# Key products of steps 1 and 2 in one 64-column matmul a unit, with ScalarE copying the diagonal blocks

## The chip, the cores and the metric

One core of a Trainium2 chip runs the whole program. The metric is device time in microseconds (us), the median of repeated runs. The kernel before takes 965.38 us (three runs, 963.65 to 966.08). The profile is of one execution of 968.78 us, whose span from first to last instruction is 967.1 us.

## The reference

Three stages follow each other: a delta-rule attention over 768 tokens (4 batches, 8 heads, head size 48), a two-layer network with a squared relu (384 to 2048 to 384), and a maxout network (three 384 to 768 products, their maximum, then 768 to 384). All in fp32.

```python
k_n = k / (np.linalg.norm(k, axis=-1, keepdims=True) + 1e-06)
for t in range(S):
    kt, vt, bt = (k_n[:, :, t], v[:, :, t], beta[:, :, t, None])
    y[:, :, t] = np.einsum('bhd,bhde->bhe', q[:, :, t], state)
    v_old = np.einsum('bhde,bhd->bhe', state, kt)
    state = state + bt[:, :, :, None] * np.einsum('bhd,bhe->bhde', kt, vt - v_old)
...
g = np.maximum(x @ w_in, 0.0) ** 2 ; x = g @ w_out
h = np.maximum(np.maximum(x @ w1, x @ w2), x @ w3) ; out = h @ w_out2
```

## The kernel before

The 768 tokens are cut into six steps t = 0 to 5 of 128 tokens, and each step into two chunks of 64. Heads go in pairs; a pair and a chunk make a unit, 32 units a step. The attention of a step is four functions. `gram(t)` forms, for each unit, the 64x64 products of the chunk's keys with each other (into the tile G) and of keys with queries (masked, into W). `solve(t)` inverts a triangular system made of G, nearly all on VectorE, with a few 32x32 matmuls at its end. `values(t)` loads v and k and scales v. `chain(t)` carries the state from chunk to chunk and writes the attention's output (`outputs`), which `split` divides into a high and a low part, xh and xl. Then `moe1(t)` runs the relu network on the step's 512 columns (four batches of 128 tokens): `hidden` with the weights wih and wil, `project` with gh, gl and the weights wo, three reduced-precision (F32R) matmuls in place of each fp32 one. In step 0 the weights are loaded raw and split into high and low parts by ScalarE and VectorE (`load_w`, tiles raw and word), and wo is written out to DRAM (wod) to be read back in later steps. The maxout network comes last.

In steps 0 to 2 (`t < BLOCKS`) `gram` loads tokens whole, transposes them on TensorE (`features`: matmuls with ident, two of 64 rows per pair), copies the result from PSUM into W on ScalarE, and makes the products eight units at a time (a batch: four batches a step). The key product of a unit is made there as two matmuls with 32 stationary columns each, the second with its two moving halves swapped, so that the diagonal 32x32 blocks of the product land in columns 0 to 31 of both row halves; that is the layout `solve` wants. Beside it stands the query product with 64 stationary columns. In steps 3 to 5 `gram` reads k and q in blocks, transposes on VectorE, and makes the key product as one 64-column matmul; ScalarE then copies the blocks of partitions 32 to 63 and 96 to 127 into place, in two pieces of up to 256 columns. Key and query products of a batch go to two PSUM banks (pk and pq), from a ring of two banks in steps 1 and 2 (ps4 and ps5, numbered ps_90 and ps_91 in the rows). The key bank is free again when ScalarE has copied it, the query bank when VectorE has multiplied it with the mask. An fp32 matmul appears as two MATMUL instructions in the trace, as one in the program's rows.

The order on each engine is a list written at build time by the `Planner`: every instruction has a due time (`pl.at`, set from tables such as GL, CL, GRAM, SOLVE, CHAIN), and a list scheduler with costs orders each engine's queue, which the engine then works off strictly in that order. So a waiting instruction holds back everything behind it on its engine. All instructions are issued from one helper line, L369; they are told apart by their tiles.

Of the kernel before, what the change touches and what calls it, by code (L numbers as in the profile page):

```python
# [53 lines left out]
class Planner:  # L54
# [3 lines left out]

    MIX, FULL, STAY, BURST, URGENT = 0.1, 21.39, 23.78, 28.69, -2.83
    INTO, BACK, RUSH = 0.12, 0.24, 3.919
    HOLD = {"vector": 0.072, "sync": 4.88}
    CHUNK, SUPPLY, AHEAD = 256, 4.0, 64
    EVENT, LANES = 0.065, 8
    LAG = {"tensor": 0.2, "vector": 0.13, "scalar": 0.15, "gpsimd": 0.08, "sync": 0.0}

# [51 lines left out]
    def forward(self, at):  # L119
# [23 lines left out]
        while todo:  # L143
# [13 lines left out]
            r = ready.get(e, [])  # L157
            hold, later = self.HOLD.get(e, 0.0), []
            while r and r[0][0] <= t + (max(self.RUSH, hold) if hold else 0.0):
# [215 lines left out]
def kernel(  # L375
# [41 lines left out]
    GB = B // 2  # L417
    EPS = 1e-6

    GL, CL, G1, DEC, BOOST, SPL, CUT, HALF, G2, LATE, BLOCKS, FIRST, HURRY = -417, 491, -55, 1170, 2515, 58, 6, 8, -218, 228, 3, 0, 0  # L420
    GRAM = (-918, 367, -1037, 1518, 303, -975)
    SOLVE = (785, -3, -777, 1402, -1665, -543)
    CHAIN = (-867, -934, 2043, 294, 401, 966)
    TICKS = 6 * NF
    W_MIN, W_MAX = 2.0 ** -15, 122876.0

# [80 lines left out]
    def tok(t, b):  # L507
        return b if t == 0 else (t * B + b) % 2
# [11 lines left out]
    def load_blocks(t, c):  # L520

        for src, dst in zip((k, q), blocks):
            sv = src.rearrange("b (a j) (t h r) d -> j t h r (b a) d", j=2, h=2, r=32)
            for h in range(2):
                for j in range(2):
                    for f0, n in ((0, 32), (32, 16)):
                        for pairs, turn in parts(t, c):
                            p0 = 64 * (j ^ turn) + f0
                            pl.sync.dma_start(
                                out=dst[p0:p0 + 32, pairs, h, 0:n],  # L530
                                in_=sv[j, 2 * t + c, h, :, pairs, f0:f0 + n],
                            )

    def load_tok(t, b, pairs=((k, kt), (q, qt))):
        i = tok(t, b)
        for src, dst in pairs:
            n = 64 if turned(t, 1, b // 2) else P
            pl.sync.dma_start(
                out=dst[i].rearrange("p a j d -> p (a j) d")[0:n, :, 0:D],
                in_=src[b, :, t * P:t * P + n, :].rearrange("h s d -> s h d"),  # L540
            )
            for j in range(2) if n < P else ():
                pl.sync.dma_start(
                    out=dst[i][n:P, :, 1 - j, 0:D],
                    in_=src[b, j:H:2, t * P + n:(t + 1) * P, :].rearrange("h s d -> s h d"),
                )
# [41 lines left out]
    def adv(n):  # L588
        pl.at += n

    def gram(t, at):

        pl.at = at + GRAM[t]
        W, G = W2[t % 2], GG[t % 2]
        a_ring = gram_ring if t > 1 else Ring(banks[4:6] if t else banks)
        def features(b, keys):
            u0, u1 = 2 * HP * b, 2 * HP * (b + 1)
            ps = a_ring().rearrange("p (a x) -> p a x", a=HP)
            src = (kt if keys else qt)[tok(t, b)]
            for a in range(HP):  # L600
                pl.tensor.transpose(
                    ps[:, a, :], src[:, a].rearrange("p j d -> p (j d)"), ident
                )
            ps = ps.rearrange("p a (c x) -> p (a c) x", c=2)
            if keys:
                pl.scalar.activation(W[:, u0:u1, 0:64], ps, AF.Copy)
            else:
                pl.scalar.activation(W[0:64, u0:u1, 64:128], ps[0:64], AF.Copy)
                pl.scalar.activation(W[64:128, u0:u1, 128:192], ps[64:128], AF.Copy)

        def products(units, keys, queries):

            n = 2 * HP
            Wu, Gu = (x[:, units] for x in (W, G))
            pk, pq = (a_ring().rearrange("p (u x) -> p u x", u=n) if x else None for x in (keys, queries))
            for x in range(n):
                with pl.together(beside=True):
                    for p0, q0, c0 in ((0, 64, 64), (64, 0, 128)):
                        key = Wu[p0:p0 + 64, x, 0:64]
                        if keys and t < BLOCKS:  # L620
                            lo, hi = key[:, 0:32], key[:, 32:64]
                            turned = bass.AP(hi.tensor, hi.offset, [list(hi.ap)[0], [-32, 2], [1, 32]])
                            for o0, lhs, rhs in ((0, lo, key), (32, hi, turned)):
                                pl.tensor.matmul(pk[p0 + o0:p0 + o0 + 32, x], lhs, rhs, start=True, stop=True)
                        elif keys:
                            pl.tensor.matmul(pk[p0:p0 + 64, x], key, key, start=True, stop=True)
                        if queries:
                            pl.tensor.matmul(
                                pq[q0:q0 + 64, x], key, Wu[p0:p0 + 64, x, c0:c0 + 64],
                                start=True, stop=True,  # L630
                            )
            if keys:
                pl.scalar.activation(Gu, pk, AF.Copy)
                for p0 in (32, 96) if t >= BLOCKS else ():
                    p = slice(p0, p0 + 32)
                    pl.scalar.activation(Gu[p, :, 0:32], pk[p, :, 32:64], AF.Copy)
                    odd = slice(1, n, 2) if units.step is None else slice(0, n * (units.start % 2))
                    if odd.stop:
                        pl.scalar.activation(Gu[p, odd, 32:64], pk[p, odd, 0:32], AF.Copy)
            if queries:  # L640
                for p0, c0 in ((64, 64), (0, 128)):
                    p = slice(p0, p0 + 64)
                    pl.vector.tensor_tensor(
                        Wu[p, :, c0:c0 + 64], pq[p],
                        mask[p].unsqueeze(1).to_broadcast([64, n, 64]), op=ALU.mult,
                    )

        if t >= BLOCKS:
            for c in range(2):
                load_blocks(t, c)  # L650
                for x, (p0, n, c0) in ((0, (0, P, 0)), (1, (0, 64, 64)), (1, (64, 64, 128))):
                    p = slice(p0, p0 + n)
                    pl.vector.transpose(
                        out=W[p, c::2, c0:c0 + 64].rearrange("p n (h r) -> p n h r", h=2), in_=blocks[x][p]
                    )
                adv(4)
                for g in range(2):
                    products(slice(NP * g + c, NP * (g + 1), 2), True, True)
                    adv(2)
            return  # L660
        for keys in ((True, False) if t == 0 else (True,)):
            for b in range(B):
                u0 = 2 * HP * b
                features(b, keys)
                if t == 0:
                    adv(1)
                    products(slice(u0, u0 + 2 * HP), keys, not keys)
                    adv(2)
                    continue
                features(b, False)  # L670
                adv(1)
                nb = t * B + b + 2
                if nb < BLOCKS * B:
                    load_tok(nb // B, nb % B)
                products(slice(u0, u0 + 2 * HP), True, True)
                adv(2)
        if t == 0:
            for b in range(2):
                load_tok(1, b)
        if t + 1 == BLOCKS:  # L680
            for x in blocks:
                for p0 in (32, 96):
                    pl.gpsimd.memset(x[p0:p0 + 32, :, :, 16:32], 0.0)

    def solve(t, at):

        pl.at, pl.rush = at + SOLVE[t], t < HURRY
        G = GG[t % 2]
# [98 lines left out]
    def chain(t, at):  # L787
        pl.at = at + CHAIN[t]
        Wp = W2[t % 2].rearrange("p (n c) x -> p n c x", c=2)
# [414 lines left out]
```

## Time and profile before

| | us |
|---|---|
| median of 3 runs | 965.38 |
| profiled execution, its time | 968.78 |
| its span | 967.1 |
| TensorE matmul busy | 929.1 (96%) |
| VectorE busy | 540.8 (56%) |
| ScalarE busy | 450.0 (47%) |
| mean granted TensorE clock | 0.934 of full speed |

Names: PE is TensorE's matmuls, PEld its weight loads, DVE VectorE, ACT ScalarE, SP the queue that issues the DMAs. A row of the timeline gives the start, the duration, the engine, the output and inputs, the shape (64\*32 is 64 contraction rows by 32 stationary columns) and, in brackets, how long the engine had been idle before and what ended that. Rows that the timeline merges carry the name of one shape. The clock is a share of the full 2.4 GHz: 1.00 is that level, 0.50 the level of 1.2 GHz.

### The profile page before, as it was taken

What the parts mean: (1) busy time and instruction counts of PE and PEld (TensorE: products, weight loads), DVE (VectorE), ACT (ScalarE), POOL (GpSimd) and SP (SyncE); (2) the same over time, 40 slices, a digit from 0 to 9 for tenths busy, and PEclk for the clock granted to TensorE, in tenths of its full rate; (3) what the DMA queues carried; (4) which work ended last, traced back from release to release, by engine and by line L of the source; (5) the groups of instructions that cost most, each with busy time, mean ns of one, the idle gap of its engine ahead of it and who ended that gap; (6) DMA issues with size and microseconds to landing.
All of it is one profiled execution on the core that took longest, in us unless ns stands there. A gap on an engine that the chain in (4) does not pass through costs nothing.

```text
span 967.1 us, 24720 instructions
## 1 busy us (share of the span) xinstructions
PE 929.1 (96%) x10540; PEld 760.3 (79%) x10540; DVE 540.8 (56%) x1325; ACT 450.0 (47%) x844; POOL 34.5 (4%) x55
## 2 busy tenths in 40 slices
PE   5689799999999999999999999999999999999998
PEld 4455698777788788887787788888898989898987
DVE  6663999553696795697496289832323232232221
ACT  6321688544346655655646588953222212121111
POOL 6000001000001001000000000000000000000000
PEclk9655699777799999999999999999999999999999
DMA  8621447732366483463334367832020100000000
GB/s 212 170 66 50 109 142 239 180 100 61 77 158 140 77 196 94 107 127 116 78 100 124 101 202 226 274 98 82 1 66 1 58 8 25 9 25 9 20 14 34
DMA packets 166895, 96.09 MB, mean 99 GB/s; under 512 B 130560, under 2 KB 146816, under 8 KB 166784
## 3 DMA queue, kind: packets, MB, share of 16 engines
q1 hardware_dynamic: 166272, 94.40, 35.9%
q8 instruction: 83, 1.36, 0.6%
q14 instruction: 28, 0.23, 0.1%
q0 software_dynamic: 512, 0.10, 0.1%
HBM read 79.53 MB, written 14.94 MB: 98 GB/s over the span
## 4 chain that ended last, share of the span: by engine, by line
PE 90%; DVE 5%; DMA 2%; ACT 2%; issue 1%; SPq 0%; DVEq 0%; ACTq 0%
PE ps L369 90%; DVE word L369 1%; DVE W L369 1%; DMA wod<-wo 1%; DMA wo<-wod 1%; DMA kt<-in_k_dram 1%; DVE L L369 1%; ACT W L369 0%; DVE T L369 0%; DVE step L369 0%; ACT G L369 0%; DVE tmp L369 0%; DVE st L369 0%; ACT word L369 0%; DVE wo L369 0%
## 5 line engine op out<-in xcount | busy, mean ns | idle before, releaser
L369 PE MATMUL ps<-gh,wo 128*128 128x512 f32 (+1 forms) x624 | 159.8, 385 | 0.8 <-DMA wo<-wod 0.7
L369 ACT ACTIVATE r<-ps 128x512 f32<-128x512 f32 (+1 forms) x140 | 80.2, 573 | 154.6 <-PE ps L369 151.1
L369 DVE TENSOR_TENSOR r<-r,ps 128x512 f32<-128x512 f32 x72 | 49.5, 688 | 178.7 <-PE ps L369 176.5
L369 PEld LDWEIGHTS ps<-gh,wo 128*128 128x128 f32 x624 | 112.3, 192 | 22.8 <-DMA wo<-wod 1.2
L369 PE MATMUL ps<-W 64*64 64x64 f32 (+1 forms) x1920 | 114.6, 256 | 9.5 <-ACT W L369 6.1
L369 PE MATMUL ps<-xh,wih 128*128 128x512 f32 (+1 forms) x312 | 122.3, 392 | 1.0 <-ACT r L369 0.7
L369 PE MATMUL ps<-xh,wil 128*128 128x512 f32 (+1 forms) x312 | 117.5, 377 | 0.0
L369 PE MATMUL ps<-xl,wih 128*128 128x512 f32 (+1 forms) x312 | 117.2, 376 | 0.0
L369 PEld LDWEIGHTS ps<-W 64*64 64x64 f32 (+1 forms) x1920 | 77.3, 138 | 50.2 <-issue 23.4
L369 DVE TENSOR_TENSOR gl<-r,gh 128x512 fp32r<-128x512 f32 (+1 forms) x104 | 67.3, 647 | 77.8 <-ACT gh L369 77.5
L369 PE MATMUL ps<-gl,wo 128*128 128x512 f32 (+1 forms) x312 | 84.6, 380 | 0.0
L369 ACT ACTIVATE G<-ps 32x256 f32<-32x256 f32 (+2 forms) x84 | 41.0, 497 | 79.4 <-PE ps L369 78.4
L369 PEld LDWEIGHTS ps<-xh,wih 128*128 128x128 f32 x312 | 59.1, 190 | 13.2 <-ACT r L369 1.1
L369 PEld LDWEIGHTS ps<-xl,wih 128*128 128x128 f32 x312 | 59.3, 190 | 10.8
L369 PEld LDWEIGHTS ps<-xh,wil 128*128 128x128 f32 x312 | 59.4, 190 | 9.0
L369 DVE TENSOR_TENSOR W<-ps,mask 64x512 f32<-64x512 f32 x48 | 33.0, 688 | 58.7 <-PE ps L369 57.9
L369 PEld LDWEIGHTS ps<-gl,wo 128*128 128x128 f32 x312 | 57.0, 191 | 11.0
L369 ACT ACTIVATE gh<-r 128x512 fp32r<-128x512 f32 (+1 forms) x104 | 62.0, 596 | 5.5 <-PE ps L369 3.2
L369 ACT ACTIVATE r<-r 128x512 f32<-128x512 f32 (+1 forms) x104 | 61.9, 596 | 2.2
L369 DVE TENSOR_SCALAR word<-word 128x384 f32<-128x384 f32 x112 | 40.7, 364 | 33.9 <-ACT word L369 32.9
L369 ACT ACTIVATE m0h<-r 128x512 fp32r<-128x512 f32 x18 | 11.4, 632 | 66.7 <-DVE r L369 66.7
L369 ACT ACTIVATE m1h<-r 128x512 fp32r<-128x512 f32 x18 | 11.4, 632 | 66.6 <-DVE r L369 66.6
(155 smaller groups left out, 1753.5 us busy)
## 6 DMA issues: line engine op xcount, KB each, us to landing
wo<-wod SPq DMA_DIRECT2D x88, 384.0 KB, 3.2
raw<-in_moe_w_out_dram SPq DMA_DIRECT2D x22, 384.0 KB, 4.0
raw<-in_moe_w_dram SPq DMA_DIRECT2D x18, 384.0 KB, 4.2
raw<-in_moe_w_in_dram SPq DMA_DIRECT2D x16, 384.0 KB, 3.7
wod<-wo SPq DMA_DIRECT2D x16, 384.0 KB, 4.1
out_dram<-ob SPq DMA_DIRECT2D x24, 192.0 KB, 1.8
x2d<-raw SPq DMA_DIRECT2D x12, 256.0 KB, 3.7
vn<-in_v_dram SPq DMA_DIRECT2D x14, 192.0 KB, 4.4
```

What stands on the lines that cost most here:

```text
L369: self.plan.add(self.name, lambda: fn(*args, **kw), cost, [out], ins, flow, late, count)
```

## The change

The condition for the two-matmul form becomes `t == 0` in place of `t < BLOCKS`, and the ScalarE copies are made for every t but 0. So in steps 1 and 2 each unit's key product is one 64-column matmul (128 fp32 matmuls fewer, 256 MATMUL instructions), and after each of the eight batches ScalarE makes four copies more out of the key bank: per row half one of all eight units (32 partitions, 8x32) and one of the four odd units (4x32). The planner's constants and the due times change as well.

```diff
-    MIX, FULL, STAY, BURST, URGENT = 0.1, 21.39, 23.78, 28.69, -2.83
+    MIX, FULL, STAY, BURST, URGENT = 0.15, 9.75, 24.6, 26.29, 0.28
...
-    GRAM = (-918, 367, -1037, 1518, 303, -975)
+    GRAM = (-977, 125, -888, 1475, 723, -985)
...
                         key = Wu[p0:p0 + 64, x, 0:64]
-                        if keys and t < BLOCKS:
+                        if keys and t == 0:
                             lo, hi = key[:, 0:32], key[:, 32:64]
...
             if keys:
                 pl.scalar.activation(Gu, pk, AF.Copy)
-                for p0 in (32, 96) if t >= BLOCKS else ():
+                for p0 in (32, 96) if t else ():
                     p = slice(p0, p0 + 32)
                     pl.scalar.activation(Gu[p, :, 0:32], pk[p, :, 32:64], AF.Copy)
```

TensorE's list before, where a batch of step 1 ends and the next begins (W_106 is step 1's W; ps_90 takes the key products, ps_91 the query products; kt and qt are the tokens that are transposed):

```order
50 L369 MATMUL ps_91<-W_106 64x64
51 L369 MATMUL ps_90<-W_106 32x64 x2
52 L369 MATMUL ps_91<-W_106 64x64
53 L369 MATMUL ps_90<-ident,kt 128x128 x4
54 L369 MATMUL ps_91<-ident,qt 128x128 x4
55 L369 MATMUL ps_90<-W_106 32x64 x2
56 L369 MATMUL ps_91<-W_106 64x64
57 L369 MATMUL ps_90<-W_106 32x64 x2
```

and the same place of the changed kernel:

```order
50 L369 MATMUL ps_91<-W_106 64x64
51 L369 MATMUL ps_90<-W_106 64x64
52 L369 MATMUL ps_91<-W_106 64x64
53 L369 MATMUL ps_91<-ident,qt 128x128 x4
54 L369 MATMUL ps_90<-ident,kt 128x128 x4
55 L369 MATMUL ps_90<-W_106 64x64
56 L369 MATMUL ps_91<-W_106 64x64
57 L369 MATMUL ps_90<-W_106 64x64
```

Every pair of 32-column matmuls has become one of 64 columns, and the transposes of the queries stand ahead of those of the keys.

ScalarE's list before, from the end of step 1's first batch to the end of the second (G_108 is step 1's G; raw, word, wih are a weight being split):

```order
42 L369 ACTIVATE G_108<-ps_90 128x512
43 L369 ACTIVATE raw_83<-raw_83 128x384
44 L369 ACTIVATE W_106<-ps_90 128x8x64
45 L369 ACTIVATE W_106<-ps_91 64x8x64 x2
46 L369 ACTIVATE raw_81<-raw_81 128x384
47 L369 ACTIVATE word_84<-raw_83 128x384
48 L369 ACTIVATE G_108<-ps_90 128x512
```

and of the changed kernel:

```order
42 L369 ACTIVATE G_108<-ps_90 128x512
43 L369 ACTIVATE raw_83<-raw_83 128x384
44 L369 ACTIVATE G_108<-ps_90 32x8x32
45 L369 ACTIVATE G_108<-ps_90 32x4x32
46 L369 ACTIVATE G_108<-ps_90 32x8x32
47 L369 ACTIVATE G_108<-ps_90 32x4x32
48 L369 ACTIVATE W_106<-ps_91 64x8x64 x2
49 L369 ACTIVATE W_106<-ps_90 128x8x64
50 L369 ACTIVATE word_84<-raw_83 128x384
51 L369 ACTIVATE raw_81<-raw_81 128x384
52 L369 ACTIVATE wih<-word_85 128x3x128
53 L369 ACTIVATE G_108<-ps_90 128x512
```

The four added copies stand between the batch's first copy and the copies into W that the next batch's products need.

In step 2 (W_105) the products stand among the relu network's matmuls; the beginning of a batch before:

```order
978 L369 MATMUL ps_89<-xh,wih 128x512
979 L369 MATMUL ps_89<-xh,wil 128x512
980 L369 MATMUL ps_89<-xl,wih 128x512
981 L369 MATMUL ps_91<-W_105 32x64 x2
982 L369 MATMUL ps_90<-W_105 64x64
983 L369 MATMUL ps_91<-W_105 32x64 x2
984 L369 MATMUL ps_90<-W_105 64x64
```

and of the changed kernel:

```order
999 L369 MATMUL ps_89<-xh,wil 128x512
1000 L369 MATMUL ps_89<-xl,wih 128x512
1001 L369 MATMUL ps_86<-gh_78,wo_101 128x512 x2
1002 L369 MATMUL ps_91<-W_105 64x64
1003 L369 MATMUL ps_90<-W_105 64x64
1004 L369 MATMUL ps_91<-W_105 64x64
```

Here too the batch is one run of equal 64-column matmuls, between network matmuls as before.

## Rows read from the trace of the kernel before

**Rows 1.** The page, part 2: VectorE and granted TensorE clock in 40 slices.
```profile
DVE  6663999553696795697496289832323232232221
...
PEclk9655699777799999999999999999999999999999
```

**Rows 2.** Windows: stretch, its length, busy us (instructions) by engine, clock, DMA share, GB/s.
```profile
36.50:96.50 60.00, 54.53 (x404) 33.74 (x404) 26.93 (x80) 12.05 (x23) 1.27 (x2) 0.50 0.28 73
96.50:118.60 22.10, 15.38 (x611) 13.99 (x610) 20.82 (x65) 16.00 (x30) 1.89 (x2) 0.64 0.44 111
118.60:177.80 59.20, 57.68 (x1098) 52.55 (x1099) 57.83 (x163) 47.98 (x111) 3.28 (x4) 1.00 0.67 196
177.80:248.00 70.20, 70.20 (x811) 48.80 (x811) 25.55 (x53) 27.32 (x55) 2.08 (x4) 0.72 0.35 89
248.00:280.00 32.00, 32.00 (x132) 26.23 (x133) 28.81 (x92) 15.72 (x28) 0.00 (x0) 0.93 0.57 136
...
340.00:967.10 627.10, 621.04 (x5698) 521.62 (x5696) 309.88 (x701) 273.48 (x495) 8.24 (x10) 1.00 0.29 84
```

**Rows 3.** Timeline, a batch of step 1's products, from 48.56 to 64.21 us.
```profile
48.56 1.11 PE L369 MATMUL ps<-ident,kt 128*128 128x128 f32 x4 [0.30 <-ACT G L369]
...
52.15 11.77 PE L369 MATMUL ps<-W 64*64 64x64 f32 x92 [0.93 <-ACT W L369]
...
52.90 0.58 PEld L369 LDWEIGHTS ps<-W 64*64 64x64 f32 x6 [0.17 <-issue]
...
63.56 0.60 ACT L369 ACTIVATE G<-ps 128x512 f32<-128x512 f32 x1 [10.42 <-PE ps L369]
64.02 0.69 DVE L369 TENSOR_TENSOR W<-ps,mask 64x512 f32<-64x512 f32 x1 [9.46 <-PE ps L369]
...
64.21 1.11 PE L369 MATMUL ps<-ident,kt 128*128 128x128 f32 x4 [0.30 <-ACT G L369]
```

**Rows 4.** Tile W, 36 to 50 us: shapes in one merged row of products.
```profile
L369 PE MATMUL ps<-W x92: 310/311/366, 36.5 to 48.0; 64*32 64x64 f32 x60, 64*64 64x64 f32 x32
```

**Rows 5.** Waits of VectorE, 36.5 to 248 us: total us, times, longest.
```profile
DVE W L369 <- PE ps L369: 47.5, 7, 9.5
```

**Rows 6.** Timeline, TensorE: step 0's queries; step 3's products; step 4's products.
```profile
23.75 1.15 PE L369 MATMUL ps<-W 64*64 64x64 f32 x32 [0.29 <-ACT W L369]
...
311.13 0.50 PE L369 MATMUL ps<-xh,wih 128*128 128x512 f32 x1
311.47 0.39 PE L369 MATMUL ps<-xh,wil 128*128 128x512 f32 x1
...
392.36 1.16 PE L369 MATMUL ps<-W 64*64 64x64 f32 x64
```

**Rows 7.** Timeline, TensorE: all product rows of step 2.
```profile
177.79 7.42 PE L369 MATMUL ps<-W 64*32 64x64 f32 x72
189.44 2.98 PE L369 MATMUL ps<-W 64*32 64x64 f32 x23
...
201.42 7.26 PE L369 MATMUL ps<-W 64*32 64x64 f32 x72
212.42 1.04 PE L369 MATMUL ps<-W 64*32 64x64 f32 x12
215.21 1.04 PE L369 MATMUL ps<-W 64*32 64x64 f32 x12
221.39 10.00 PE L369 MATMUL ps<-W 64*32 64x64 f32 x96
238.02 9.77 PE L369 MATMUL ps<-W 64*32 64x64 f32 x96
```

**Rows 8.** Groups of ScalarE by shape: count, busy us, mean ns.
```profile
L369 ACT ACTIVATE G<-ps 32x256 f32<-32x256 f32 x36 | 13.0, 375 | 0.7
```

**Rows 9.** Chain that ended last: start, us, what.
```profile
118.04 0.48 DVE xl L369
118.56 15.46 PE ps L369 x282
```

**Rows 10.** Waits of TensorE on the weights that are read back, whole run.
```profile
PE ps L369 <- DMA wo<-wod: 0.7, 1, 0.7
```

More of the change, by code (lines that the diff above doesn't have):

```diff
@@ L54 @@
 class Planner:
-    MIX, FULL, STAY, BURST, URGENT = 0.1, 21.39, 23.78, 28.69, -2.83
-    INTO, BACK, RUSH = 0.12, 0.24, 3.919
-    HOLD = {"vector": 0.072, "sync": 4.88}
-    CHUNK, SUPPLY, AHEAD = 256, 4.0, 64
+    MIX, FULL, STAY, BURST, URGENT = 0.15, 9.75, 24.6, 26.29, 0.28
+    INTO, BACK, RUSH = 0.12, 0.24, 3.659
+    HOLD = {"vector": 0.091, "sync": 10.65}
+    CHUNK, SUPPLY, AHEAD = 256, 4.0, 160
     EVENT, LANES = 0.065, 8
@@ L418 @@
     EPS = 1e-6
-    GL, CL, G1, DEC, BOOST, SPL, CUT, HALF, G2, LATE, BLOCKS, FIRST, HURRY = -417, 491, -55, 1170, 2515, 58, 6, 8, -218, 228, 3, 0, 0
-    GRAM = (-918, 367, -1037, 1518, 303, -975)
-    SOLVE = (785, -3, -777, 1402, -1665, -543)
-    CHAIN = (-867, -934, 2043, 294, 401, 966)
+    GL, CL, G1, DEC, BOOST, SPL, CUT, HALF, G2, LATE, BLOCKS, FIRST, HURRY = -327, 520, -50, 1215, 2684, 111, 6, 8, -295, 228, 3, 0, 0
+    GRAM = (-977, 125, -888, 1475, 723, -985)
+    SOLVE = (537, -135, -737, 1294, -1608, -366)
+    CHAIN = (-629, -1055, 2137, 252, 294, 828)
     TICKS = 6 * NF
```

## The prediction

> **What bounds the kernel now.** I read the page's slices first. The granted clock is at 0.5 to 0.7 in two stretches, from about 36 to 115 us and from about 180 to 255 us, and 1.00 elsewhere; VectorE is nearly idle in much of both, and nearly full between them [rows 1]. Then a table by stages. From 340 us on TensorE is busy 621.0 of 627.1 us at clock 1.00: that part is bound by TensorE, and a microsecond that the beginning saves comes off the end. From 36.5 to 96.5 us it is busy 54.5 of 60 us too, but at clock 0.50 and with 404 instructions only, while VectorE works 26.9 us and ScalarE 12.1 us; from 177.8 to 248.0 us it is busy throughout at a mean of 0.72 [rows 2]. The timeline says with what: the key and query products of steps 1 and 2, 11.77 us for a batch of 96 instructions (92 recorded) at half clock [rows 3]. The merged row hides two shapes, 64 instructions of 32 stationary columns and 32 of 64 [rows 4]. Their weight loads come in sixes, 0.58 us of loads and then 0.17 us in which the loads stand still for nothing else that the trace shows [rows 3]: six instructions are half a unit (two key matmuls, one query matmul), and 0.753 us (52.90 less 52.15) times 16 halves is 12.05 us.
>
> Behind each batch ScalarE waits for its G copy (10.42 us) and VectorE for its mask (9.46 us) [rows 3], and what VectorE could do meanwhile, the solve of step 0 and the splitting of weights, stands behind that mask in its list. In all it waits 47.5 us for products between 36.5 and 248 us, in seven waits [rows 5].
>
> Where the program makes the products with 64 columns only, in step 4, a batch of 64 instructions takes 1.16 us at clock 1.00, 18 ns each: the four quadrants of the array run beside each other. Step 0's queries, two quadrants only, take 36 ns each (1.15 us for 32) [rows 6].
>
> **The change part by part.** (A) Step 1's four batches. At half clock the new batch costs 2 x 1.16 = 2.3 us. Bounds: 1.16 us if the clock is up, and 64 x 0.125 = 8.0 us if nothing overlaps (0.753 / 6 is the old price of one instruction). I take 2.3, the rate of the same shapes in the same order in step 4. Added are four ScalarE copies a batch: two of 32x256 at 375 ns [rows 8] and two of 32x128, which the trace doesn't show; between 0 and 375 ns, I take 300, near the shown one: 1.35 us. They hold the key bank, and the next keys' transposes wait for that; the query transposes now stand ahead of them and fill that wait. A batch took 15.65 us from key transposes to key transposes (64.21 less 48.56) [rows 3]; now 15.65 - 11.8 + 2.3 + 1.35 = 7.5 us. The last batch ended at 96.4 us; now at about 36.5 + 2.3 + 3 x 7.5 = 61, 35 us earlier. But then VectorE is next. Up to the first network matmul at 118.56 us, which waits for a VectorE operation that ends at 118.5 (xl) [rows 9], it has 26.9 + 20.8 = 47.7 us of work in 82.1 us [rows 2], and its list ahead of that xl is the same but for the order. At 95% busy that takes 50.3 us, so the network begins near 87 us, 32 us earlier. I take 30, with 20 (VectorE at 77%) and 34 (never idle) as ends.
>
> (B) Step 2's four batches. Their rows sum to 39.5 us [rows 7], in a stretch in which TensorE never rests. New: 4 x 1.16 = 4.6 us, 34.9 less. Clock: 0.72 over 70.2 us is 39.3 us at the half level. The old products at full clock would be 4 x 6.0 = 24.1 us (half of 12.05), so 2 x (39.5 - 24.1) = 30.8 us of the half-clock time lay in them and 8.5 us on network and chain matmuls; at full clock these get back 4.2 us. In step 4, where short runs of products stand between network matmuls, the clock stays at 1.00 [rows 2], so I count that too: 39 us. If the clock falls as before, the products cost 9.3 and nothing comes back: 30 us. With nothing overlapped at half clock it would be 39.5 - 32 = 7.5 us.
>
> One rule of the Trainium skill speaks against the cheap batch. The trace first: step 4's 18 ns against 36 ns with two quadrants [rows 6] says that the upper and the lower key product of a unit, which write the same PSUM bank, do overlap. The page TensorEngine Tiling (Array Packing), section Restrictions and Gotchas, says that different row tiles cannot access the same bank simultaneously. By that rule two quadrants at most would run at once, 2.3 us a batch at full clock, and B would be 4.6 us and A some 9 us smaller; step 4's rows contradict it, so the sum doesn't use it.
>
> (C) The new list goes from network matmuls to fp32 ones and back 62 times in place of 72. Coming back costs 0.11 us (0.34 us between the first two network matmuls after products, against 0.23 elsewhere) [rows 6]; with as much on the way in, 10 x 0.2 = 2 us.
>
> (D) What is late next. From 118.6 to 280 us VectorE works 57.8 + 25.6 + 28.8 = 112.2 us of 161.4 [rows 2]. With B and C gone the stretch has 120 us: 93% busy. ScalarE has 91.0 us and 5.4 of new copies: 80%. The work is mostly the splitting of step 0's weights and solve(1), which can't be put off. From 118.6 to 177.8 us VectorE was at 98% already and TensorE lost 1.5 us, so such a load can be carried; but queues worked off in order seldom keep two engines full for 120 us. I take a loss of 7 us, with 0 and 25 as ends (25 is VectorE at 77%, as in A). The added copies of step 2 cost TensorE nothing: network matmuls stand beside them; uncovered they would cost 4 x 1.35 = 5.4 us, inside that range.
>
> The remaining tables move work of steps 3 to 5 inside a stretch that TensorE fills to 99% [rows 2]: nothing to win, and I count no loss.
>
> Sum: 967.1 - 30 - 39 - 2 + 7 = 903.1 us of span, 904.8 us of time (1.7 us lie around the span). The profiled execution stands 3.4 us above the median of the runs (968.78 against 965.38); less that, 901.4. I forecast **902 us**.
>
> **Rivals.**
> Likeliest, 72%: the sum. Its own range is 888 (A 34, B 39, C 3, D 0) to 914 (A 25, B 36, D 12).
>
> VectorE takes over, 18%: weights come too late and TensorE waits for them between 90 and 200 us. For it: 93% asked of an in-order engine. Against it: the 98% that it carried before. At A 20, B 39, C 2 and D 25 the span is 931, the time about 929; midway, 920.
>
> The clock stays low in step 2, 7%: the products still come in runs of quarter-array matmuls, and before the change every long run of them stands at 0.5. Against it: steps 3 to 5. B is then 30: about 911 us.
>
> Slower or unchanged, 3%. The weights that are read back come late: the tables for their due times and for the DMA queue change, and a ring of four holds them. Before, TensorE's matmuls waited 0.7 us for them in all [rows 10], with 88 such loads. To eat 63 us each load would have to make TensorE wait 0.72 us. From there it decides; at 0.9 us each the time is 902 + 79 = 981 us. That the change doesn't do what it says (64-column products as dear as the mix) belongs here too: at 0.125 us an instruction A would give at most 15 and B 7.5 us, some 940 us, still faster.
>
> **How the numbers follow.** The range is 886 to 926: it holds the likeliest case, the clock case and half of VectorE's. A measurement here can tell about 0.3% (3 us) from no change. Faster needs only a tenth of A and B: 96%. Slower 3%, the same 1%.
>
> **What would show it.** Right: batches of 64 instructions of 64 columns in steps 1 and 2, near 2.3 and 1.2 us; the first network matmul at 85 to 92 us; the clock at 1.00 from there on; VectorE's wait for products below 15 us; step 0's network done some 65 us earlier; the stretch behind it as long as before. Wrong: a batch over 4 us; a clock below 0.9 between 100 and 250 us; TensorE waiting more than 10 us for split weights or for VectorE; waits on weights read back in steps 1 to 5.

## The result and the profile after

The changed kernel takes 900.77 us (median of 4 runs, 899.16 to 903.26) against 964.79 us for the kernel before: a ratio of 0.9338, 95% interval 0.9312 to 0.9364. The forecast was 902 us. The profiled execution has a span of 901.3 us, 65.8 us shorter.

The page's slices of the kernel after, to be held against [rows 1]:

```profile
DVE  6999998689479749957923898323324131413131
...
PEclk9756999999999999999999999999999999999999
```

The second stretch of low clock is gone and the first ends some 30 us sooner; VectorE, at three to six tenths in the first before, is at nine tenths from the second slice to the sixth.

The stages, cut where the same work ends (columns as in [rows 2]):

```profile
36.50:85.40 48.90, 31.84 (x886) 27.93 (x886) 48.05 (x147) 32.49 (x68) 3.19 (x4) 0.53 0.55 143
85.40:134.00 48.60, 48.45 (x822) 45.98 (x819) 48.05 (x142) 39.85 (x92) 3.17 (x4) 0.98 0.62 195
134.00:182.20 48.20, 43.56 (x1000) 35.18 (x999) 35.51 (x73) 41.14 (x88) 2.33 (x4) 0.96 0.65 166
...
274.20:901.30 627.10, 616.69 (x5735) 519.29 (x5733) 308.52 (x699) 268.54 (x487) 8.24 (x10) 1.00 0.29 83
```

From 36.5 us to the first network matmul it was 82.1 us and is 48.9; VectorE is busy in 48.05 of these 48.9, and bounds the stage. The last 627.1 us hold nearly what they held before [rows 2], with 4.3 us more in which TensorE stands idle (616.7 against 621.0 busy). In the stretch from 134 to 182.2 us TensorE loses another 4.6 us, and VectorE is not the reason: it is busy for 35.5 of 48.2 us.

TensorE's and its neighbours' timeline around a batch of step 1, which answers to [rows 3], and the first network matmul (start, duration, engine, what, idle time before):

```profile
42.50 1.11 PE L369 MATMUL ps<-ident,qt 128*128 128x128 f32 x4 [3.68 <-DVE W L369]
...
45.52 1.98 PE L369 MATMUL ps<-W 64*64 64x64 f32 x64 [1.05 <-ACT W L369]
...
47.55 1.72 ACT L369 ACTIVATE G<-ps 128x512 f32<-128x512 f32 x5 [0.78 <-PE ps L369]
...
48.50 0.70 DVE L369 TENSOR_TENSOR W<-ps,mask 64x512 f32<-64x512 f32 x1
...
49.32 1.12 PE L369 MATMUL ps<-ident,kt 128*128 128x128 f32 x4 [1.82 <-ACT G L369]
51.10 1.11 PE L369 MATMUL ps<-ident,qt 128*128 128x128 f32 x4 [0.66 <-DVE W L369]
53.50 1.98 PE L369 MATMUL ps<-W 64*64 64x64 f32 x62 [0.88 <-ACT W L369]
...
85.45 0.58 PE L369 MATMUL ps<-xh,wih 128*128 128x256 f32 x1
```

A batch is 1.98 us at half clock where it was 11.77. It is now TensorE that waits, for ScalarE's copies (the five of a batch merged into one row of 1.72 us) and for VectorE's mask. VectorE hardly waits for products any more. Its waits for them from 36.5 to 248 us (total, times, longest):

```profile
DVE W L369 <- PE ps L369: 1.5, 2, 0.9
```

It was 47.5 us in seven waits [rows 5]. Step 2's batches, which answer to [rows 7]; the two at 156 us are one batch:

```profile
145.59 1.16 PE L369 MATMUL ps<-W 64*64 64x64 f32 x64
156.10 0.25 PE L369 MATMUL ps<-W 64*64 64x64 f32 x2
156.17 1.14 PE L369 MATMUL ps<-W 64*64 64x64 f32 x62
171.22 1.16 PE L369 MATMUL ps<-W 64*64 64x64 f32 x64
180.35 1.16 PE L369 MATMUL ps<-W 64*64 64x64 f32 x64
```

Some 4.7 us in all against 39.5, with the clock near 1.00. What is new stands in TensorE's waits from 100 us to the end:

```profile
PE ps L369 <- issue: 11.6, 10, 3.2
```

In the kernel before, the waits put down to issue were 3.6 us from 100 us on. The second longest of the new ones, in the timeline (the longest, 3.15 us up to 458.36 us, also stands behind a run of small matmuls):

```profile
159.05 2.00 PE L369 MATMUL ps<-W,US 128*32 128x64 f32 x128
160.98 0.33 PE L369 MATMUL ps<-ident,qt 128*128 128x128 f32 x1
164.32 0.55 PE L369 MATMUL ps<-ident,qt 128*128 128x128 f32 x3 [3.01 <-issue]
```

The second of four equal transposes starts 3 us late, with nothing to wait for: the fourfold group is cut in the middle, right behind 128 small matmuls in 2 us.

### The profile page after: what moved, and what is told of

Same layout as the page of the kernel before. It is cut to its first block, busy times and chain, and to the rows that moved or that the text cites. A ratio compares the mean times of both kernels' runs of the same rounds, so it can differ in the third digit from the quotient of the medians.

```text
span 901.3 us, 24239 instructions
## 1 busy us (share of the span) xinstructions
PE 849.2 (94%) x10284; PEld 717.2 (80%) x10284; DVE 541.1 (60%) x1325; ACT 459.4 (51%) x876; POOL 35.0 (4%) x55
## 4 chain that ended last, share of the span: by engine, by line
PE 83%; DVE 11%; ACT 3%; issue 2%; DMA 1%; DVEq 0%; ACTq 0%
PE ps L369 83%; DVE word L369 3%; ACT G L369 2%; DVE step L369 1%; DVE T L369 1%; DMA raw<-in_moe_w_in_dram 1%; DVE W L369 1%; DVE F L369 1%; DVE L L369 1%; DVE tmp L369 1%; DVE G L369 0%; DVE wo L369 0%; DVE gl L369 0%; ACT word L369 0%; DVE st L369 0%
## 5 line engine op out<-in xcount | busy, mean ns | idle before, releaser
L369 DVE TENSOR_TENSOR r<-r,ps 128x512 f32<-128x512 f32 x72 | 49.6, 688 | 178.7 <-PE ps L369 176.5
L369 PE MATMUL ps<-gh,wo 128*128 128x512 f32 (+1 forms) x624 | 154.8, 377 | 1.3 <-ACT G L369 1.3
L369 PEld LDWEIGHTS ps<-xl,wih 128*128 128x128 f32 x312 | 59.7, 191 | 10.9
L369 ACT ACTIVATE G<-ps 32x256 f32<-32x256 f32 (+3 forms) x116 | 50.1, 447 | 15.9 <-PE ps L369 14.5
L369 DVE TENSOR_SCALAR word<-word 128x384 f32<-128x384 f32 (+1 forms) x112 | 41.5, 373 | 18.0 <-ACT word L369 16.7
L369 PE MATMUL ps<-W 64*64 64x64 f32 (+1 forms) x1664 | 40.4, 238 | 10.3 <-ACT W L369 5.4
L369 PEld LDWEIGHTS ps<-W 64*64 64x64 f32 (+1 forms) x1664 | 34.8, 145 | 17.8 <-issue 8.4
L369 ACT ACTIVATE ob<-ps 128x384 f32<-128x384 f32 x24 | 11.8, 492 | 58.3 <-PE ps L369 58.3
```

The source lines that it names most:

```text
L369: self.plan.add(self.name, lambda: fn(*args, **kw), cost, [out], ins, flow, late, count)
```

## The experiments

All ratios are against runs of the kernel before on the same chip, the changed kernel's being 0.9338.

**The form alone, and the tables alone.** The first kernel is the one before with the two conditions of the change, the second the changed kernel with the two conditions of before.

```diff
-                        if keys and t < BLOCKS:
+                        if keys and t == 0:
...
-                for p0 in (32, 96) if t >= BLOCKS else ():
+                for p0 in (32, 96) if t else ():
```

> The new form (64-column key products and the ScalarE copies in steps 1 and 2) with the tables and planner constants of before. My theory: nearly all of the gain is the form; 900 to 912 us, batches of 64 instructions near 2.0 us in step 1 and 1.2 us in step 2. Rival: the new due times are what lets the network fill the freed time; then 920 us or more, with TensorE waiting between 60 and 250 us.

> The old form with the new tables and constants. My theory: the tables alone move little, 960 to 970 us, with the batches at 11.8 us and the clock at 0.5 as before. Rival (the tables carry a part of the gain): 950 us or less.

Measured: the form alone 907.43 us, ratio 0.9366 (0.9327 to 0.9404); the tables alone 975.06 us, 1.0083 (1.0050 to 1.0117). The form brings the whole gain, within the intervals. The tables by themselves cost 0.8%, which the expectation of 960 to 970 missed; what they add to the new form (0.9338 against 0.9366) is not resolved.

**One step alone.** The changed kernel with the old form back in step 2 or in step 1.

```diff
-                        if keys and t == 0:
+                        if keys and t in (0, 2):        # the other kernel: (0, 1)
...
-                for p0 in (32, 96) if t else ():
+                for p0 in (32, 96) if t not in (0, 2) else ():
```

> The changed kernel with the old form back in step 2, so that only term A is left. My theory: A is 30 to 33 us, so 930 to 936 us, the network begins near 85 us and the clock falls again in step 2's products. Rival (VectorE, not the products, sets the pace after 87 us): step 2's slow products then cost less than in the kernel before, and the time is below 925 us.

> The changed kernel with the old form back in step 1, so that only term B is left. My theory: B less its losses is 32 to 38 us, so 926 to 933 us; the two single gains add up to the whole one within 6 us. Rival (the two gains share one limit, VectorE): each alone is larger, and their sum exceeds the whole gain of 64 us by 10 us or more.

Measured: step 1 alone 940.86 us, ratio 0.9726 (0.9691 to 0.9760); step 2 alone 939.58 us, 0.9713 (0.9676 to 0.9751). Both lie above what I expected, by 5 and 7 us from the upper ends. I had counted from the kernel before; the base of both is the kernel with the tables alone, at 1.0083. From there step 1 brings 0.0357, step 2 0.0370, together 0.0727; both at once bring 0.0745. In microseconds of a 966 us run these are 34.5, 35.7, 70.2 and 72.0. So the two terms add up, and the rival, one shared limit on VectorE, falls. The network was expected near 85 us with step 1 alone; it begins at 93.88 us, 27.6 us before the 121.43 of the tables alone, and the gain is 34.5 us all the same. So the start of the network is not the whole measure of a gain: TensorE had done more instructions by then (1079 recorded from 36.5 to 93.8 us, against 886 to 85.4 us in the changed kernel). With step 1 alone, step 2 looks as it did before:

```profile
150.00:220.00 70.00, 70.00 (x873) 50.49 (x873) 30.11 (x61) 30.02 (x60) 2.09 (x4) 0.72 0.40 94
```

This is a stage of the kernel with step 1 alone: the clock at 0.72, TensorE busy throughout, VectorE with 30 of 70 us of work. It is the products that bring the clock down: the same stretch of network and chain work stands near 1.00 without the mix (0.96 from 134 to 182.2 us of the changed kernel, 1.00 in the 32 us behind).

**Is it the 32-column matmul or the alternation?** The kernel before, where in steps 1 and 2 a batch makes all key products (still two 32-column matmuls a unit, no added copies), and then all query products.

```diff
-            for x in range(n):
+            apart = 0 < t < BLOCKS
+            for x, first, second in (
+                [(x, True, False) for x in range(n)] + [(x, False, True) for x in range(n)]
+                if apart else [(x, True, True) for x in range(n)]
+            ):
...
-                        if keys and t < BLOCKS:
+                        if keys and first and t < BLOCKS:
...
-                        if queries:
+                        if queries and second:
```

> The kernel before (its tables too), with steps 1 and 2 still at two 32-column key matmuls a unit and no ScalarE copies, but all eight units' key products of a batch first, and then all its query products: the two shapes no longer alternate. My theory: it is the alternation of shapes that costs; a batch then takes 64 x 21 + 32 x 36 ns = 2.5 us at full clock and 4 to 5 us at half, and the time is 905 to 920 us. Rival: the 32-column matmuls are slow whatever stands beside them (0.125 us each at half clock); then a batch stays above 8 us in step 1 and the time above 945 us.

> The same grouping of the old form with the new tables and constants. Theory as for the run before: 902 to 918 us, within 8 us of the changed kernel. Rival: above 945 us.

Measured: 908.36 us, ratio 0.9378 (0.9349 to 0.9406), with the old tables, and 913.69 us, 0.9439 (0.9408 to 0.9471), with the new. The timeline of the first, in step 1, at half clock:

```profile
40.67 1.97 PE L369 MATMUL ps<-W 64*64 64x64 f32 x32 [1.28 <-ACT W L369]
...
46.18 1.93 PE L369 MATMUL ps<-W 64*32 64x64 f32 x64 [0.69 <-ACT W L369]
```

64 key instructions take 1.93 us and 32 query instructions 1.97 us: 3.9 us for the same 96 instructions that took 11.77 when the two shapes alternated. Both rows lie in a stretch at a clock of 0.50 throughout (36.5 to 62 us). This settles what is slow: not the 32 stationary columns, but going from one shape to the other and back in every half unit. The turn from one PSUM bank to the other is not it, since the changed kernel makes it too and takes 1.98 us a batch. What in the change of shape costs the time stays open. Removing the alternation by order alone, with no change of layout and no copies, gives as much as the change did under the tables of before (0.9378 against 0.9366). Under the new tables it gives less: 913.69 us is 13 us above the changed kernel, outside the 8 us that I expected, and the intervals are apart (0.9408 to 0.9471 against 0.9312 to 0.9364). The network begins at 93.49 us there, in place of 85.45, with one wait of 11.1 us for VectorE (its tile Tn) before it.

**What the ScalarE copies cost.** They can't be left out, since the solve reads what they write; so they are made twice.

```diff
-                for p0 in (32, 96) if t else ():
+                for p0 in (32, 96, 32, 96) if 0 < t < BLOCKS else (32, 96) if t else ():
```

> The changed kernel with the four ScalarE copies of every batch of steps 1 and 2 made twice (32 copies more, same values). My theory: VectorE sets the pace in step 1 and TensorE in step 2, so the copies are covered: 0 to 4 us more, 901 to 905. Rival: they stand on the path (they hold the key bank and the next keys' transposes): 8 x 1.1 = 9 us more or over.

Measured: 911.58 us, ratio 0.9409 (0.9379 to 0.9439), 0.0071 or 7 us above the changed kernel. It lies between the two expectations, nearer to the rival: copies made twice are not covered. (The planner also orders the lists anew for them, so part of the 7 us may be order.) In step 1 the network begins at 86.75 us in place of 85.45; the rest is lost later, where TensorE now waits for ScalarE's part of the network. Its waits from 100 us on:

```profile
PE ps L369 <- issue: 10.4, 11, 2.1
PE ps L369 <- ACT r L369: 3.8, 5, 1.7
```

**Less of a burst.** The changed kernel with the planner's constant AHEAD of before.

```diff
-    CHUNK, SUPPLY, AHEAD = 256, 4.0, 160
+    CHUNK, SUPPLY, AHEAD = 256, 4.0, 64
```

> The changed kernel with one planner constant of before, AHEAD 64 in place of 160, which lets fewer small matmuls follow each other before network matmuls are put between. My theory: the waits of TensorE that the profile puts down to issue (14.4 us in the changed kernel, 5.0 before) follow bursts of small matmuls, so they fall to 5 to 9 us, and the time to 895 to 900. Rival: they don't come from bursts; they stay above 12 us and the time at 900 or more.

Measured: 906.33 us, ratio 0.9355 (0.9321 to 0.9389). From 100 us on the waits put down to issue fall from 11.6 to 5.3 us:

```profile
PE ps L369 <- issue: 5.3, 9, 1.2
```

But over the whole run they are 10.9 us, more than the 5 to 9 expected, and the time is not the 895 to 900 expected, nor lower than the changed kernel's (the intervals overlap). The network begins at 88.46 us here, 3 us later, which takes back part of it; where the rest went stays open.

**A burst by itself.** The changed kernel, with each batch of products of step 5 made eight times in one run that nothing may be put into.

```diff
+            if t == NS - 1:
+                with pl.together():
+                    for x in list(range(n)) * 8:
+                        ...
```

> The changed kernel with each batch of products of step 5 made eight times in one unbroken run (512 MATMUL instructions and as many weight loads; the same values each time). If small matmuls are bound by TensorE alone, a batch takes 512 x 17 ns = 8.7 us with no idle time inside, and the run 4 x 7.6 = 30 us more. My theory for the waits called issue: instructions run out in a long burst of small ones; then the burst stops after some hundreds of instructions with gaps put down to issue, and its mean is well over 17 ns each, at 25 ns or more (13 us a batch).

Measured, in a single run: 950.39 us, with 30.9 us of waits put down to issue. That is 49.6 us above the changed kernel, where TensorE alone would have made it 30 and the 13 us a batch of the theory some 47. Inside a batch (TensorE's timeline):

```profile
447.75 2.09 PE L369 MATMUL ps<-W 64*64 64x64 f32 x128 [1.12 <-issue]
451.22 2.09 PE L369 MATMUL ps<-W 64*64 64x64 f32 x128 [1.38 <-issue]
454.69 2.10 PE L369 MATMUL ps<-W 64*64 64x64 f32 x128 [1.38 <-issue]
458.16 0.27 PE L369 MATMUL ps<-W 64*64 64x64 f32 x2 [1.38 <-issue]
```

128 matmuls and their 128 weight loads, 256 instructions, run in 2.09 us, and then TensorE stands for 1.38 us, in a period of 3.47 us: 27 ns a matmul in place of 17. This is the last of the four batches, 13.9 us long (444.54 to 458.43 us), near the 13 us of the theory. The transfers hardly run meanwhile (the stretch from 445 to 450 us, products' instructions only; the last two columns are the DMA share and GB/s of the core):

```profile
445.00:450.00 5.00, 3.73 (x239) 1.00 0.03 7
```

So the gaps are no effect of other traffic: in a long run of small matmuls, instructions come in blocks of 256 at about 3.5 us each. The DMA queues of the trace show the blocks. The queue named instruction moves 95 packets in this run and 81 in the changed kernel, for 27825 and 24239 instructions on all engines: 14 packets more for 3586 instructions more, 256 a packet. In the three periods from 447.75 to 458.16 us it moves three, and no other queue moves any:

```profile
q8 instruction: 3, 0.05, 1.8%
```

By the times of the single packets in the trace, TensorE starts again 1.3 to 1.4 us after each of the three has landed. The same holds in the changed kernel: each of its ten waits put down to issue from 100 us on ends 1.2 to 1.5 us after such a packet has landed, though on average one comes only every 11 us (81 in 901.3 us). So those waits are waits for instructions. Why a packet is not fetched sooner, the runs don't show.

**Two candidates.** Step 1 as changed, step 2 with 32 columns, grouped and without copies, under either set of tables.

```diff
+            apart = t == 2
...
-                        if keys and t == 0:
+                        if keys and first and t in (0, 2):
...
```

> A candidate: the changed kernel with step 2 back at 32-column key matmuls, but grouped (all keys of a batch, then all queries) and without the ScalarE copies there; step 1 as changed. If the copies in step 2 cost what doubling them suggests (some 3 us for one step), 897 to 901 us; if the queue order decides at this level, anywhere between 898 and 912.

> The same forms with the tables of before: 899 to 910 us; below 903 only if the copies in step 2 are on the path.

Measured: 905.83 us, ratio 0.9359 (0.9315 to 0.9403), and 902.73 us, 0.9331 (0.9292 to 0.9370). Neither can be told from the changed kernel; the second reaches it with the tables of before. It lies 0.3 us under the mark of 903 that was to show the copies of step 2 on the path, which is too little to show it: its interval overlaps that of the form alone (0.9327 to 0.9404), which makes those copies under the same tables.

## Why the prediction was right, point by point

- **The cause** was named rightly: the mixed batches, their half clock, and VectorE's list held up behind them. The prediction priced the new batch by step 4's rows without saying why the mix was slow; the grouped run shows that it is the alternation of shapes. The rule on PSUM banks of the Trainium skill (the page TensorEngine Tiling (Array Packing), section Restrictions and Gotchas), which the prediction weighed and left out of its sum, would have made a batch 2.3 us at full clock. The trace does not agree: step 2's batches take 1.16 us.
- **(A)** Forecast 30 us with VectorE as the next bound at 95% busy; measured 33.1 (118.56 to 85.45 us), at 98%. A batch period of 7.5 us was forecast; the products start at 36.84, 45.52, 53.50 and 60.88 us, 8.7, 8.0 and 7.4 us apart. The new batch takes 1.98 us at half clock (2.3 forecast), the four copies 1.12 us (1.72 less 0.60; 1.35 forecast). What the prediction had wrong inside the period is the query transposes, which were to fill the wait for the key bank: the first of them wait 3.68 us for VectorE's mask themselves, and in the next batch they come behind the key transposes. The gain by the step alone is 34.5 us.
- **(B)** Products 39.5 to 4.7 us as forecast, and the clock at 0.96 to 1.00 where it was 0.72. The gain by the step alone, with its share of the losses, is 35.7 us; B was 39 before losses.
- **(C), (D)** The rest of the span, 65.8 - 33.1 = 32.7 us, is to be held against B + C - D = 34. From the first network matmul to the end TensorE's busy time falls by 42.3 us (840.7 to 798.4; B + C was 41), and its idle time grows by 9.6 us (7.8 to 17.4; D was 7). D's size held nearly, its place did not. I had named VectorE at 93% as what is late next, before 280 us. From 85.4 to 134 us it was busy for 48.05 of 48.6 us and TensorE still lost only 0.15 us. The losses are 4.6 us between 134 and 182 us (1.5 from 118.6 to 177.8 us before), some 2 us more than before between 214 and 274 us, and 4.3 us more after 274 us, where I counted none; VectorE is far from full in all three. 11.6 us of TensorE's waits from 100 us on are put down to issue, and the packets of instructions show what they are: runs of small instructions too dense for their supply. The form alone takes these waits from 3.6 to 9.0 us, the tables alone to 6.8. The prediction did not count that. (Two slips besides: the lower end of the likeliest case, A 34, B 39, C 3, D 0, adds up to 889 us, not 888; and VectorE was not nearly idle in the stretches of low clock, but busy for 26.9 of 60 us and 25.6 of 70.2 [rows 2].)
- **The added copies** were costed at nothing in step 2. Doubling them in both steps costs 7 us, so this was probably too favourable: made once, they may cost something of that order in the two steps together, though the kernels without them in step 2 were not measurably faster.
- **The rivals.** VectorE taking over: no, shown by the two single steps, whose gains add up. The clock staying low in step 2: no, it is up as soon as the mix is gone (0.96 to 1.00); in step 1 it is still 0.53, with TensorE idle for 17 of 48.9 us. Weights read back late: TensorE's matmul waits from 100 us on name no such load.

## What to carry to other kernels

Look for short matmuls of different tile shapes in alternation: here they cost 11.77 us for 96 instructions where the same instructions, sorted by shape, took 3.9. Try sorting them before changing the layout; it needs no other engine, and under the tables of before it gave as much. When a stretch shows TensorE busy at low clock, price its work by rows of the same shapes at full clock elsewhere in the run, and look at which engine's list stands behind it.

## What the runs showed of the hardware

- Matmuls with 32 and with 64 stationary columns in turn: 0.753 us for six instructions at half clock [rows 3], that is 125 ns each; in runs of one shape 30 ns (1.93 us for 64 of 32 columns) and 62 ns (1.97 us for 32 of 64 columns, two quadrants), at the same clock.
- In unbroken runs of small matmuls TensorE's instructions arrive in blocks: 256 instructions (one packet of the instruction queue, by the counts of the two runs above) run in 2.09 us, then a gap of 1.38 us, in each of three successive periods of 3.47 us, with the transfers at a share of 0.03. Gaps of 3.01 and 3.15 us came where other transfers were running (share 0.88 from 161.0 to 164.3 us, 0.63 from 455.2 to 458.4 us); that their traffic lengthened them was not tried.
- Four quadrants with two row halves writing one PSUM bank ran at 18 ns a matmul in step 2's four batches of the changed kernel, at a clock of 1.00; two quadrants took 36 ns [rows 6].
